# A third score buffer, token rows whole in DRAM, and a TensorE turn for the early expert slots

## The chip, the cores and the metric

The kernel runs on one core of a Trainium2 chip. Its time is device time in microseconds (us) of that core, and lower is better.

## The reference

Queries are mean-pooled in pairs before attention; the attention output, laid out as tokens, goes through a top-1 mixture of experts.

```python
B, H, S, D = (8, 8, 1152, 64)
q_pool = q.reshape(B, H, S // 2, 2, D).mean(axis=3)          # 576 queries
scores = (1 / sqrt(D)) * q_pool @ k.T                         # 576 x 1152 a head
attn = exp(scores - max); attn /= attn.sum(-1) + 1e-09
x = (attn @ v).transpose(0, 2, 1, 3).reshape(4608, 512)       # tokens
logits = x @ w_gate                                           # 8 experts
expert_idx = argmax(logits);  gate_w = softmax(logits)[expert_idx]
for e in range(8):                                            # 512 -> 1024 -> 512
    out[mask] = gate_w[mask] * (relu(x[mask] @ w1[e]) @ w2[e])
```

## The kernel before, in words

One Python class, `Flow`, plans the whole program. Each step is added with an engine, a cost in ns, a key (its due place), the steps it follows and the buffers it holds (`room` says how many of each kind there are). `Flow` plays the steps through with these costs and writes every engine's instructions in the order that comes out. On the chip each engine runs its own list in that order and waits at semaphores, so a step that waits holds up all that stands behind it on its engine.

**Attention** runs over 8 batches, in each over 4 pairs of heads, in each over 2 halves of 288 queries. A half is 9 chunks of 128 keys. For each chunk TensorE forms scores for both heads in a score buffer `st` of two PSUM banks (`product`, L516), and VectorE takes them to the tile `s` and finds their maxima in the same pass (`take`, L520); this frees the buffer. After the last chunk TensorE spreads the maxima into a further `st` buffer (L538), VectorE makes the bias (L544), ScalarE takes the exponential in three pieces (L548). The product with V collects 9 chunks in `pa`, two PSUM banks (L619); ScalarE and VectorE bring it to `xT` (L623, L624). For the softmax sums (`chunk_sum`) GpSimd folds nine chunks to two in three additions (L594) and TensorE adds those over the keys (L603), or, for the last half of a batch and for three pairs of the last batch, TensorE adds all nine (L589). All eight halves of a batch accumulate in one PSUM bank, `sums`. `row_sums` brings that bank to SBUF (ScalarE, L633), turns it (L639) and inverts it (L645, L646). `routing` computes logits, picks the expert, ranks tokens and scatters list entries (L793), in the same `sums` bank. PSUM has 8 banks: two `st` buffers of two, `pa` two, `sums` one, `m` one.

The rows of tokens go to DRAM in `x_runs`: a token's 512 values are four runs of 128 values and its factors, 528 bytes each. The four planes of runs lie one behind the other, so a token's runs are far apart. SyncE stores them with one DMA per third of a batch (L785).

**Experts** run in slots: 3 early ones (L818 onwards picks them after batch 6), 6 wide ones of 384 tokens, and a static rest. For a slot GpSimd loads its list (L877, L879), forms indices (L888; VectorE does for early slots) and gathers the runs, 128 runs an indirect DMA (L892), twelve for 384 tokens. VectorE multiplies by the softmax factors (L1051) and turns the tokens with a 32x32 block transpose (L1054), which with the four planes on four groups of partitions gives the transposed matrix; ScalarE and VectorE split it into a high and a low part, `xh` (L1058) and `xl` (L1015). Weights are split the same way (L1075, L1015). TensorE forms the hidden layer in three products (L1107) and the output in three (L1134); ScalarE scales it (L1146), GpSimd scatters it (L1141).

Of the kernel before, what the change touches and what calls it, by code (L numbers as in the profile page):

```python
# [9 lines left out]
F32 = mybir.dt.float32  # L10
# [12 lines left out]
S_BUFS = 2  # L23
BANKS = 5 - S_BUFS * 2
UNITS = 4
# [228 lines left out]
def kernel(  # L254
# [43 lines left out]
    planes = xg.rearrange("(g t) x -> g t x", g=NQD)  # L298
# [52 lines left out]
    for g in range(NQD):  # L351
        nc.vector.memset(gid[g * BL:(g + 1) * BL], float(g * (NT + 1)))
# [47 lines left out]
    def open_attention(exact, base, pairs, units):  # L400
# [3 lines left out]
        o.ps_m = base.enter_context(tc.tile_pool(name="ps_m", bufs=3 if exact else BANKS, space=PSUM))  # L404
# [19 lines left out]
    def turn_ns(n):  # L424
        return 60 + 1.25 * n
# [14 lines left out]
    def sum_bank(o):  # L440
        return hold_of("sums", lambda h: o.ps_m.tile([P, 512], F32, **h.own("sums", 1)))
# [57 lines left out]
    def scores(o, f, key, x, half, step=None):  # L499
# [8 lines left out]
        for c in range(NC):  # L508
            pt = hold_of("st", lambda h: o.ps_s.tile([P, 2, 512], F32, **h.own("st")))
# [15 lines left out]
            m = f.add("PE", 460, product, at, done(*x.q[half], *x.k.get(c, ())), [pt, s, x.kT, x.qT], QUADS)  # L525
            taken.append(f.add("DVE", 150 + dve(2 * HQ), take, at, done(m), [pt, s]))
# [5 lines left out]
        pb = hold_of("st", lambda h: o.ps_s.tile([P, 2, 512], F32, **h.own("st")))  # L532
# [45 lines left out]
    def chunk_sum(o, f, key, s, ready, b, hp, half, sums, last):  # L578


        key += K_SUM
        if not o.exact and (hp == NHP - 1 and half == 1 or b == B - 1 and hp >= NHP - LAST):

            def whole():
                for i in range(0, NC, 2):
                    for j in range(min(2, NC - i)):
                        for h in range(2):
                            to = slice(64 * j + 32 * h, 64 * j + 32 * h + 32)
                            nc.tensor.matmul(sums.t[to, :HQ], ones4[:, hp, half, :], s.t[:, i + j, h], start=False,  # L589
                                             stop=hp == NHP - 1 and half == 1 and i + j + 2 >= NC, tile_position=(0, to.start))  # L590

            return f.add("PE", 485 * (NC + 1) // 2, whole, key + 10, [*every(ready), *done(*last)], [s, sums], COLS)
        u = tile_of(o, "fold", [P, 3, 2, HQ], bufs=FOLD_BUFS, pool=o.rt)
        add = lambda to, a, b: nc.gpsimd.tensor_tensor(to, a, b, ALU.add)  # L594
        p = f.add("POOL", pool(6 * HQ), lambda: add(u.t, s.t[:, 0:3], s.t[:, 3:6]), key, every(ready[:6]), [s, u])
        p = f.add("POOL", pool(6 * HQ), lambda: add(u.t, u.t, s.t[:, 6:9]), key, done(p, *every(ready[6:])), [s, u])
        p = f.add("POOL", pool(2 * HQ), lambda: add(u.t[:, 0], u.t[:, 0], u.t[:, 2]), key, done(p), [u])

        def total():
            for i in range(2):  # L600
                for h in range(2):
                    to = slice(64 * i + 32 * h, 64 * i + 32 * h + 32)
                    nc.tensor.matmul(sums.t[to, :HQ], ones4[:, hp, half, :], u.t[:, i, h], start=hp == half == 0,  # L603
                                     stop=hp == NHP - 1 and half == 1, tile_position=(0, to.start))

        return f.add("PE", 500, total, key + 15, done(p, *last), [u, sums], COLS)

    def values(o, f, key, x, s, ready, hp, half, xT):
        pa = hold_of("pa", lambda h: o.ps_m.tile([P, 2, 512], F32, **h.own("pa", 1)))
# [3 lines left out]
        for c in range(NC):  # L613
# [8 lines left out]
            p = f.add("PE", 460, product, key + 20.0 * c / NC, done(p, x.v, ready[c]), [pa, x.vn, s], QUADS)  # L622
# [4 lines left out]
    def row_sums(o, f, key, sums, summed, rec, sm, end):  # L627

        key += K_ROW - end * 30
        if end and FILL:  # L630
            f.add("PE", 215 * FILL, lambda: [nc.tensor.matmul(
                sums.t[:, 3 * P:], ones, ones, start=True, stop=True) for _ in range(FILL)], key, summed, [sums])
        p = f.add("ACT", act(HQ) - 44, lambda: nc.scalar.copy(sm.t, sums.t[:, :HQ]), key, summed, [sums, sm])  # L633
# [3 lines left out]
        def turn():  # L637
            for j in range(HQ // QP):
                nc.tensor.matmul(sums.t[:QP, HQ + j * NS:HQ + (j + 1) * NS], sm.t[:, j * QP:(j + 1) * QP],  # L639
                                 sums_of.rearrange("p f a h -> p (f a h)"), start=True, stop=True)  # L640

        def inverse():

            src = sums.t[:QP, HQ:HQ + 3 * NS].rearrange("p (j f h) -> p f j h", j=3, f=2)
# [3 lines left out]
        p = f.add("PE", 500, turn, key, done(p), [sm, sums])  # L648
        return f.add("DVE", 600, inverse, key, done(p), [sums, rec])

    def attend(o, f, key, b, hp, xT, sums, summed):
# [3 lines left out]
        for half in range(2):  # L655
            at = key + 20 * half
            s, r = scores(o, f, at, x, half, EXPS)
            summed.append(chunk_sum(o, f, at + 20, s, r, b, hp, half, sums, summed[-1:]))
# [5 lines left out]
    def routing(o, f, key, b, xT, rec, sums, ready, hold=()):  # L664
# [18 lines left out]
        pl = pt = pr = sums  # L683

        aside = lambda at, n: pt.t[:QP, 3 * P + at:3 * P + at + n]
# [4 lines left out]
        def logits():  # L690
            for half in range(2):
                for a in range(NHP):
                    nc.tensor.matmul(
                        pl.t[32 * a:32 * a + 32, :HQ], wg[:, a, half, :], xT.t[:, a, half * HQ:(half + 1) * HQ],
# [524 lines left out]
    with tc.If(again > 0):  # L1219
        reset_state()  # L1220
        empty_lists()
        with ExitStack() as cm:
            o = open_attention(True, cm, cm, cm)
            with tc.For_i(0, B, 1) as b:
# [6 lines left out]
                for hp in range(NHP):  # L1231
                    attend(o, f, 0, b, hp, xT, sums, [])
# [49 lines left out]
```

## Time and profile before

| | us |
|---|---|
| median of 3 runs (range) | 1287.85 (1286.34 to 1294.69) |
| the profiled execution | 1292.46 |
| its span in the trace | 1290.9 |
| mean granted TensorE clock in it | 0.972 of full speed |

The span is what the trace covers; 1.56 us lie around it. The profiled execution is 4.6 us above the median. Attention fills the span to about 799 us, batch by batch, and the experts the rest.

### The profile page before, as it was taken

To read this page: it belongs to the slowest core of one execution; us is meant where nothing else is said; L and a number is where in the kernel's file an instruction comes from. 1 tells how busy PE (TensorE), PEld (TensorE's weight loads), DVE (VectorE), ACT (ScalarE), POOL (GpSimd) and SP (SyncE) were. 2 spreads that over 40 slices of the span, in tenths; PEclk is the share of its full clock that TensorE was granted. 3 is DMA by queue.
4 is the path that set the end of the run, shared out by engine and by line. 5 is a ranking of instruction groups with operands and counts; after the bars stand their busy time and mean duration, and the time that the engine had idled before them with its cause. 6 is when DMAs were issued, how large, how long until landed. Compare 5 with 4: busy or idle time off the path is not lost. (4 is left out here: it accounts for less than half of the span.)

```text
span 1290.9 us, 32856 instructions
## 1 busy us (share of the span) xinstructions
PE 1178.6 (91%) x13393; PEld 807.8 (63%) x13393; DVE 888.5 (69%) x2241; ACT 594.2 (46%) x688; POOL 809.3 (63%) x491
## 2 busy tenths in 40 slices
PE   4899999999999998999998496997999999999997
PEld 1455555455455454554554143886898899998986
DVE  5788877878878879788877243874556656566661
ACT  1455455445455445454552134443444444455551
POOL 0897699697795995996991622255887886421000
PEclk9899999999999999999999689998999999999999
DMA  9874446456456447555452301675566565566640
GB/s 146 127 116 88 104 66 108 99 92 96 83 92 107 88 83 125 76 89 111 76 94 82 110 18 40 159 224 148 175 186 185 176 181 173 159 223 193 232 149 20
DMA packets 379585, 158.12 MB, mean 122 GB/s; under 512 B 311012, under 2 KB 346780, under 8 KB 379424
## 3 DMA queue, kind: packets, MB, share of 16 engines
q1 hardware_dynamic: 367440, 135.10, 47.5%
q0 software_dynamic: 10896, 20.78, 5.8%
q8 instruction: 108, 1.77, 0.6%
q14 instruction: 53, 0.43, 0.1%
q10 hardware_dynamic: 1088, 0.03, 0.1%
HBM read 135.06 MB, written 22.07 MB: 122 GB/s over the span
## 5 line engine op out<-in xcount | busy, mean ns | idle before, releaser
L520 DVE TENSOR_SCALAR_CACHE_REDUCE s<-st 128x576 f32<-128x576 f32 x576 | 421.6, 750 | 138.2 <-PE st L516 118.6
L548 ACT ACTIVATE s<-s,bias 128x1728 f32<-128x1728 f32 x192 | 326.0, 1731 | 361.5 <-DVE bias L544 297.0
L516 PE MATMUL st<-qT,kT 64*64 64x288 f32 x4608 | 378.5, 417 | 55.7 <-DVE s L520 26.0
L619 PE MATMUL pa<-s,vn 64*64 64x288 f32 x4608 | 358.9, 406 | 4.1 <-issue 2.9
L516 PEld LDWEIGHTS st<-qT,kT 64*64 64x64 f32 x4608 | 161.1, 134 | 205.2 <-DVE s L520 86.6
L619 PEld LDWEIGHTS pa<-s,vn 64*64 64x64 f32 x4608 | 172.1, 134 | 107.5 <-issue 20.2
L594 POOL TENSOR_TENSOR fold<-s 128x1728 f32<-128x1728 f32 x51 | 197.0, 3869 | 22.9 <-ACT s L548 22.7
L594 POOL TENSOR_TENSOR fold<-fold,s 128x1728 f32<-128x1728 f32 x51 | 197.1, 3870 | 0.9
L1107 PE MATMUL ph<-xh,w1h 128*128 128x384 f32 (+1 forms) x512 | 163.4, 319 | 17.8 <-DVE hl L1115 8.2
L1107 PE MATMUL ph<-xl,w1h 128*128 128x384 f32 (+1 forms) x512 | 161.6, 316 | 0.2 <-DVE xl L1015 0.2
L1107 PE MATMUL ph<-xh,w1l 128*128 128x384 f32 (+1 forms) x512 | 161.3, 315 | 0.0
L892 POOL DMA_INDIRECT xr<-x_runs,ix x104 | 115.1, 1107 | 63.0 <-DVE ix L888 32.9
L1141 POOL DMA_INDIRECT out_dram<-y,rec x41 | 48.7, 1188 | 166.8 <-ACT y L1146 143.6
L1134 PE MATMUL py<-w2h,hh 128*128 128x512 f32 x328 | 128.2, 391 | 0.0
L1134 PE MATMUL py<-w2l,hh 128*128 128x512 f32 x328 | 127.9, 390 | 0.0
L1134 PE MATMUL py<-w2h,hl 128*128 128x512 f32 x328 | 127.9, 390 | 0.0
L793 POOL DMA_INDIRECT lists<-re,di x48 | 44.5, 928 | 131.5 <-DVE di L754 122.6
L1015 DVE TENSOR_TENSOR w2l<-raw,w2h 128x1024 fp32r<-128x1024 f32 x64 | 77.9, 1221 | 65.1 <-ACT w2h L1075 38.3
L1113 ACT ACTIVATE hh<-ph 128x384 fp32r<-128x384 f32 (+1 forms) x100 | 52.0, 521 | 137.1 <-PE ph L1107 108.9
L1107 PEld LDWEIGHTS ph<-xh,w1h 128*128 128x128 f32 x512 | 97.9, 191 | 22.6 <-DVE hl L1115 10.4
L1115 DVE SCALAR_TENSOR_TENSOR hl<-ph,hh 128x384 fp32r<-128x384 f32 (+1 forms) x100 | 59.1, 592 | 60.3 <-ACT hh L1113 50.6
L1107 PEld LDWEIGHTS ph<-xl,w1h 128*128 128x128 f32 x512 | 97.8, 191 | 1.3 <-DVE xl L1015 0.6
(172 smaller groups left out, 1358.3 us busy)
## 6 DMA issues: line engine op xcount, KB each, us to landing
raw<-in_moe_w_dram SPq DMA_DIRECT2D x128, 512.0 KB
kp<-in_k_dram SPq DMA_DIRECT2D x128, 144.0 KB
qn<-in_q_dram SPq DMA_DIRECT2D x128, 144.0 KB
vn<-in_v_dram SPq DMA_DIRECT2D x128, 144.0 KB
x_runs<-row SPq DMA_DIRECT2D x24, 396.0 KB
xr<-x_runs,ix POOLq DMA_INDIRECT x104
x_runs<-empty SPq DMA_DIRECT2D x4, 297.0 KB
xq<-x_runs,ix POOLq DMA_INDIRECT x60
```

The lines of the kernel that those rows point to most:

```text
L516: nc.tensor.matmul(pt.t[to, h, :HQ], x.kT.t[up, c * P + i * D:c * P + (i + 1) * D], x.qT.t[up, cols], start=True, stop=True, tile_position ...
L520: nc.vector.tensor_scalar(s.t[:, c], pt.t[:, :, :HQ], -SCALE, None, op0=ALU.mult, op1=ALU.min, accum_out=mx.t[:, c:c + 1],)
L548: nc.scalar.activation(s.t[:, c0:c0 + n], s.t[:, c0:c0 + n], AF.Exp, bias=bias.t, scale=-1.0)
L594: add = lambda to, a, b: nc.gpsimd.tensor_tensor(to, a, b, ALU.add)
L619: nc.tensor.matmul(pa.t[cs, i, :HQ], x.vn.t[up, h, c, :], s.t[up, c, h], start=c == 0, stop=c == NC - 1, tile_position=(up.start, cs.start))
L892: nc.gpsimd.indirect_dma_start(out=x.xr[i // NQD].t[:, i % NQD, :], out_offset=None, in_=xg, in_offset=bass.IndirectOffsetOnAxis(ap=x.ix.t ...
L1015: (nc.gpsimd if eng == "POOL" else nc.vector).tensor_tensor(lo, raw, hi.bitcast(F32), ALU.subtract)
L1107: nc.tensor.matmul(view()[:, i, :], a[:, c, fp], b[:, c, :n], start=c == 0 and k == 0, stop=c == NDC - 1 and k == 2)
L1113: a = f.add("ACT", act(nb * n) - 44, lambda fs=fs, view=view: nc.scalar.activation(hidden(m)[0][:, fs, :n], view(), AF.Relu), at - 20, don ...
L1115: d = f.add("DVE", dve(nb * n), lambda fs=fs, view=view: nc.vector.scalar_tensor_tensor(hidden(m)[1][:, fs, :n], view(), 0.0, hidden(m)[0] ...
L1134: nc.tensor.matmul(py.t, a[:, c, hs], b[:, c % 2, :], start=c == 0 and k == 0, stop=c == NFC - 1 and k == 2)
L1141: nc.gpsimd.indirect_dma_start(out=out, out_offset=bass.IndirectOffsetOnAxis(ap=x.re.t.bitcast(I32)[:, r, 0:1], axis=0), in_=y.t, in_offse ...
```

## The change

1. `S_BUFS` is 3. The two single banks `sums` and `m` are gone: 3 x 2 + 2 = 8 banks. Each half's sums now go to an `st` buffer of their own; ScalarE copies the first of a batch to SBUF (`sm`), VectorE adds the seven others there. `row_sums`, `routing` (save that of the last batch, which uses `pa`'s banks), the pick of the early slots and the warm-up hold an `st` buffer too. Planner costs change: a score or value product 460 to 485 ns, `take` by 150 less, and a few of routing's.
2. In `x_runs` a token's four runs lie side by side, 2112 bytes. A third of a batch is stored by four DMAs, one per plane. The other slots gather single runs as before, by index 4 x token + plane.
3. An early slot gathers whole rows, 128 tokens a gather, with the list's own entries as indices: three gathers for 384 tokens. The multiplication writes tokens in the order that suits a full transpose (`across`, L1085 of the new file); TensorE turns 128 tokens by four 128x128 transposes into PSUM (L1092); ScalarE (L1097) and VectorE split from there.
4. In a list load the half that the gather of single runs needs (`li`) now stands behind the other (`rec2`).

The core of the diff:

```diff
-S_BUFS = 2
-BANKS = 5 - S_BUFS * 2
+S_BUFS = 3
...
-    planes = xg.rearrange("(g t) x -> g t x", g=NQD)
+    planes = xg.rearrange("(t g) x -> g t x", g=NQD)
+    whole_rows = xg.rearrange("(t g) x -> t (g x)", g=NQD)
...
-            m = f.add("PE", 460, product, at, done(*x.q[half], *x.k.get(c, ())), [pt, s, x.kT, x.qT], QUADS)
-            taken.append(f.add("DVE", 150 + dve(2 * HQ), take, at, done(m), [pt, s]))
+            m = f.add("PE", 485, product, at, done(*x.q[half], *x.k.get(c, ())), [pt, s, x.kT, x.qT], QUADS)
+            taken.append(f.add("DVE", dve(2 * HQ), take, at, done(m), [pt, s]))
...
-    def chunk_sum(o, f, key, s, ready, b, hp, half, sums, last):
+    def chunk_sum(o, f, key, s, ready, b, hp, half, sm, last):
         key += K_SUM
+        ps = score_banks(o)
...
+                        nc.tensor.matmul(ps.t[to, 0, :HQ], ones4[:, hp, half, :], u.t[:, i, h], start=True,
+                                         stop=True, tile_position=(0, to.start))
+            p = f.add("PE", 500, total, key + 15, done(p), [u, ps], COLS)
+        if not last:
+            return f.add("ACT", act(HQ) - 44, lambda: nc.scalar.copy(sm.t, ps.t[:, 0, :HQ]), key + 15, done(p), [ps, sm])
+        return f.add("DVE", dve(HQ), lambda: nc.vector.tensor_tensor(sm.t, sm.t, ps.t[:, 0, :HQ], ALU.add),
+                     key + 15, done(p, *last), [ps, sm])
...
-        pl = pt = pr = sums
+        pl = pt = pr = value_banks(o) if b == B - 1 else score_banks(o)
...
-                nc.sync.dma_start(out=rows.rearrange("d (i g j) x -> g d i (j x)", g=NB, j=NJ)[g], in_=row.t.rearrange("p j x -> p (j x)"))
+                for d in range(NQD):
+                    nc.sync.dma_start(out=rows[d].rearrange("(i g j) x -> g i j x", g=NB, j=NJ)[g], in_=row.t[d * BL:(d + 1) * BL])
...
+        if early:
+            def fetch(r):
+                nc.gpsimd.indirect_dma_start(
+                    out=x.xr[r].t.rearrange("p b x -> p (b x)"), out_offset=None, in_=whole_rows,
+                    in_offset=bass.IndirectOffsetOnAxis(ap=x.re.t.bitcast(I32)[:, r, 0:1], axis=0),
...
+            if x.whole:
+                def across(r=r, feats=feats, xt=xt):
+                    nc.vector.tensor_tensor(xt.t.rearrange("p c (d i) -> p d c i", i=BL), feats(),
+                                            x.xr[r].t[:, :, P:].unsqueeze(3).broadcast_to([P, NQD, NDC, BL]), ALU.mult)
+                px = hold_of("py", lambda h: m.ps.tile([P, DM], F32, **h.own("py")))
+                def cross(xt=xt, px=px):
+                    for c in range(NDC):
+                        nc.tensor.transpose(px.t[:, c * P:(c + 1) * P], xt.t[:, c], ident)
+                made = lambda px=px: px.t.rearrange("p (c t) -> p c t", c=NDC)
+                p = f.add("DVE", dve(DM), across, key + r, x.rows[r:r + 1], [xt, x.xr[r]])
+                p = f.add("PE", 450, cross, key + r, done(p), [x.x, px, xt])
...
```

Three places of the instruction order. First TensorE in a steady stretch of the third batch (`st` score products, `pa` value products, four instructions a chunk). Before:

```order
L619 MATMUL pa_2665<-s_2292,vn_2087 64x288 x4
L516 MATMUL st_2706<-qT_2505,kT_2281 64x288 x4
L619 MATMUL pa_2665<-s_2292,vn_2087 64x288 x8
L516 MATMUL st_2730<-qT_2505,kT_2281 64x288 x4
L619 MATMUL pa_2665<-s_2292,vn_2087 64x288 x4
L538 MATMUL st_2742<-ident,top 64x64 x4
L619 MATMUL pa_2665<-s_2292,vn_2087 64x288 x8
L516 MATMUL st_2759<-qT_2505,kT_2281 64x288 x4
L516 MATMUL st_2764<-qT_2505,kT_2281 64x288 x4
```

and after, where `st_2579` and `st_2586` are the sums of two halves in score buffers:

```order
L519 MATMUL st_2523<-qT_2071,kT_2074 64x288 x4
L519 MATMUL st_2528<-qT_2071,kT_2074 64x288 x4
L519 MATMUL st_2534<-qT_2071,kT_2074 64x288 x4
L519 MATMUL st_2541<-qT_2071,kT_2074 64x288 x4
L519 MATMUL st_2547<-qT_2319,kT_2327 64x288 x4
L628 MATMUL pa_2553<-s_2198,vn_1853 64x288 x16
L608 MATMUL st_2579<-fold_2340,ones_73 32x288 x4
L593 MATMUL st_2586<-s_2198,ones_73 32x288 x18
L541 MATMUL st_2616<-ident,top 64x64 x4
L628 MATMUL pa_2553<-s_2198,vn_1853 64x288 x4
L519 MATMUL st_2628<-qT_2319,kT_2327 64x288 x4
```

Score products now stand up to five in a row, value products up to four, and the sums stand between them in the same ring of buffers.

Second GpSimd behind the list scatters of batch 6. Before (`xr`, `xq` are the gathered tiles):

```order
L892 DMA xr_8897<-x_runs,ix_8890 128x132 x4
L892 DMA xr_8973<-x_runs,ix_8890 128x132 x4
L892 DMA xr_9036<-x_runs,ix_8890 128x132 x4
L892 DMA xr_9110<-x_runs,ix_8906 128x132 x4
L892 DMA xr_9179<-x_runs,ix_8906 128x132 x4
L892 DMA xr_9242<-x_runs,ix_8906 128x132 x4
L892 DMA xr_9305<-x_runs,ix_9102 128x132 x4
L892 DMA xq_9456<-x_runs,ix_9102 128x132 x4
L892 DMA xq_9495<-x_runs,ix_9102 128x132 x4
```

and after:

```order
L903 DMA xr_9177<-x_runs,rec_0_8916 128x528
L903 DMA xr_9182<-x_runs,rec_0_8916 128x528
L903 DMA xr_9192<-x_runs,rec_0_8916 128x528
L903 DMA xr_9205<-x_runs,rec_1_8927 128x528
L903 DMA xr_9223<-x_runs,rec_1_8927 128x528
L903 DMA xr_9242<-x_runs,rec_1_8927 128x528
L903 DMA xr_9269<-x_runs,rec_2_8938 128x528
L903 DMA xq_9564<-x_runs,rec_2_8938 128x528
L903 DMA xq_9575<-x_runs,rec_2_8938 128x528
```

Thirty-six gathers have become nine, each of 128 whole rows.

Third ScalarE where attention ends. Before (`w1h`, `w2h` are high parts of weights, `xh` of the first slot's tokens):

```order
L1075 CAST w1h_9453<-raw_8761 128x1024
L1058 CAST xh<-xt_9451 128x4x128
L1058 CAST xh<-xt_9460 128x4x128
L1075 CAST w1h_9470<-raw_8771 128x1024
L1075 CAST w1h_9478<-raw_8778 128x1024
L1075 CAST w1h_9486<-raw_8790 128x1024
L1058 CAST xh<-xt_9481 128x4x128
L623 COPY xT_8432<-pa_9375 128x288
```

and after:

```order
L1123 CAST w1h_9561<-raw_8871 128x1024
L1123 CAST w1h_9570<-raw_8876 128x1024
L1123 CAST w1h_9580<-raw_8881 128x1024
L1123 CAST w1h_9583<-raw_8883 128x1024
L1123 CAST w2h_9587<-raw_8886 128x1024
L632 COPY xT_8629<-pa_9483 128x288
L1123 CAST w2h_9597<-raw_8900 128x1024
L1097 CAST xh<-py_9591 128x4x128
L1097 CAST xh<-py_9600 128x4x128
L1123 CAST w2h_9619<-raw_9516 128x1024
L1097 CAST xh<-py_9614 128x4x128
```

The first slot's tokens come behind six weight pieces and a copy, where one weight piece stood ahead of the first two and four ahead of the third. On TensorE the twelve transposes and the logits of the last batch now stand between the last value products and the first expert product; on GpSimd the first three list loads of the wide slots have moved from behind the third scatter of the first slot's output (L1141) to between the three scatters.

## Rows read from the trace of the kernel before

**Rows 1.** The page's first part: busy time of each engine over the whole span, its share of it, and its instructions.

```profile
PE 1178.6 (91%) x13393; PEld 807.8 (63%) x13393; DVE 888.5 (69%) x2241; ACT 594.2 (46%) x688; POOL 809.3 (63%) x491
```

**Rows 2.** Four stretches of 90 us, one batch of attention each (the first of the four, and their sum): length, busy time of each engine with its count of records, granted clock, DMA share.

```profile
320.00:410.00 90.00, 85.43 (x1348) 47.49 (x1343) 73.55 (x219) 45.62 (x48) 74.52 (x31) 0.98 0.54 95
...
sum 360.00, PE 339.56 PEld 189.07 DVE 294.15 ACT 182.16 POOL 297.95; mean PE 84.89 PEld 47.27 DVE 73.54 ACT 45.54 POOL 74.49
```

**Rows 3.** Waits from 120 to 680 us, a little over six batches: engine and line, what it waited for, us in total, times, longest.

```profile
DVE s L520 <- PE st L516: 87.5, 167, 2.1
PEld st L516 <- DVE s L520: 56.0, 100, 1.4
PE st L516 <- DVE s L520: 14.1, 32, 0.9
PE sums L603 <- POOL fold L594: 6.7, 13, 1.3
POOL lists L793 <- DVE di L754: 71.0, 6, 12.1
```

**Rows 4.** Groups of instructions by line, shapes apart: line, engine, operation, tiles, count | busy, mean ns of one | idle time before. The last row is the summary of line 785's DMA issues (ns min/median/max, first and last start).

```profile
L520 DVE TENSOR_SCALAR_CACHE_REDUCE s<-st 128x576 f32<-128x576 f32 x576 | 421.6, 750 | 138.2 <-PE st L516 118.6 <-remote 17.3 <-issue 0.4
L624 DVE TENSOR_TENSOR xT<-xT,pa 128x288 f32<-128x288 f32 x64 | 28.6, 447 | 10.3 <-ACT xT L623 7.9 <-issue 2.4
L892 POOL DMA_INDIRECT xr<-x_runs,ix x104 | 115.1, 1107 | 63.0 <-DVE ix L888 32.9 <-issue 29.0 <-POOL ix L888 0.6
L1141 POOL DMA_INDIRECT out_dram<-y,rec x41 | 48.7, 1188 | 166.8 <-ACT y L1146 143.6 <-issue 13.3 <-DVE xq L1051 6.1
L1058 ACT CAST xh<-xt 128x512 fp32r<-128x512 f32 x41 | 23.7, 618 | 4.5 <-issue 2.9 <-DVE xt L1054 1.5
L700 PE MATMUL sums<-ident,sm 128*96 128x128 f32 x24 | 4.3, 286 | 0.1
L785 SPq DMA_DIRECT2D x_runs<-row x24: 537/594/1864, 137.6 to 829.0; - x24
```

**Rows 5.** Stretches of the last batch and of the passage to the experts, columns as in rows 2.

```profile
690.00:698.00 8.00, 4.96 (x58) 2.36 (x55) 6.66 (x41) 1.47 (x1) 5.51 (x6) 1.00 0.05 8
718.00:751.00 33.00, 12.80 (x72) 4.14 (x72) 3.93 (x11) 3.46 (x3) 22.07 (x22) 0.57 0.22 48
751.00:773.00 22.00, 21.54 (x296) 10.29 (x292) 13.07 (x37) 7.33 (x6) 4.01 (x4) 0.94 0.06 14
773.00:785.00 12.00, 8.58 (x91) 3.37 (x83) 3.05 (x8) 5.39 (x4) 8.02 (x8) 1.00 0.22 46
799.00:805.00 6.00, 0.67 (x1) 0.29 (x1) 5.05 (x8) 6.00 (x9) 0.00 (x0) 0.69 0.37 90
805.00:880.00 75.00, 74.15 (x386) 66.23 (x386) 57.81 (x127) 37.23 (x62) 32.03 (x32) 0.98 0.67 179
```

**Rows 6.** Timelines of single engines from 715 to 752 us (start, length, engine, line, operation, tiles, count, and in brackets the idle time before it and its releaser): the first and the last of the 24 gathers of this burst, then VectorE and TensorE.

```profile
715.38 1.04 POOL L892 DMA_INDIRECT xr<-x_runs,ix  x1 [18.02 <-DVE ix L888]
...
745.51 1.00 POOL L892 DMA_INDIRECT xr<-x_runs,ix  x1 [0.30 <-issue]
...
742.61 0.29 DVE L544 TENSOR_REDUCE bias<-st 128x1 f32<-128x128 f32 x1 [13.45 <-remote]
...
722.20 0.34 PE L538 MATMUL st<-ident,top 64*64 64x64 f32 x8 [1.94 <-issue]
...
729.21 1.24 PE L516 MATMUL st<-qT,kT 64*64 64x288 f32 x8 [2.51 <-DVE s L520]
742.96 1.24 PE L516 MATMUL st<-qT,kT 64*64 64x288 f32 x8 [12.51 <-issue]
```

**Rows 7.** TensorE beside the last eight gathers of slot 2 (773 to 784 us), columns as in rows 6.

```profile
779.33 0.68 PE L589 MATMUL sums<-s,ones 128*32 128x288 f32 x3 [0.82 <-issue]
```

**Rows 8.** TensorE and ScalarE where attention ends and the experts begin, columns as in rows 6.

```profile
794.18 4.60 PE L619 MATMUL pa<-s,vn 64*64 64x288 f32 x72
...
798.84 1.04 ACT L1075 CAST w1h<-raw 128x1024 fp32r<-128x1024 f32 x1 [5.33 <-PE pa L619]
...
800.83 2.93 ACT L1075 CAST w1h<-raw 128x1024 fp32r<-128x1024 f32 x3
...
804.34 0.69 PE L1107 MATMUL ph<-xh,w1h 128*128 128x384 f32 x1 [5.56 <-ACT xh L1058]
...
809.72 0.64 PEld L693 LDWEIGHTS sums<-xT,wg 128*32 128x32 f32 x16 [0.25 <-issue]
```

**Rows 9.** GpSimd, VectorE and TensorE around the first slot that is not an early one, columns as in rows 6, and two stretches, columns as in rows 2.

```profile
851.92 1.49 POOL L1141 DMA_INDIRECT out_dram<-y,rec  x1 [6.09 <-DVE xq L1051]
853.52 0.79 POOL L877 DMA_DIRECT2D li<-lists  x1
...
861.13 1.09 POOL L892 DMA_INDIRECT xr<-x_runs,ix  x1 [0.31 <-issue]
...
883.13 0.69 DVE L1051 TENSOR_TENSOR xr<-xr 128x512 f32<-128x512 f32 x1 [4.38 <-DMA xr<-x_runs,ix]
...
885.48 0.69 PE L1107 MATMUL ph<-xh,w1h 128*128 128x384 f32 x1 [4.94 <-DVE hl L1115]
...
880.00:886.00 6.00, 1.06 (x6) 0.74 (x5) 2.87 (x5) 1.80 (x3) 0.00 (x0) 0.77 0.65 216
900.00:904.00 4.00, 2.04 (x6) 2.04 (x7) 2.78 (x4) 0.00 (x0) 3.09 (x4) 0.54 0.24 51
```

More of the change, by code (lines that the diff above doesn't have):

```diff
@@ L403, in open_attention @@
         o.wk = base.enter_context(tc.tile_pool(name="wk", bufs=1 if exact else 2))
-        o.ps_m = base.enter_context(tc.tile_pool(name="ps_m", bufs=3 if exact else BANKS, space=PSUM))
+        o.ps_m = base.enter_context(tc.tile_pool(name="ps_m", bufs=3 if exact else 1, space=PSUM))
         o.ld = pairs.enter_context(tc.tile_pool(name="ld", bufs=1))
@@ L588, in whole @@
                             to = slice(64 * j + 32 * h, 64 * j + 32 * h + 32)
[L589 to L604, printed above, removed]
@@ L606, in chunk_sum, with total @@
-        return f.add("PE", 500, total, key + 15, done(p, *last), [u, sums], COLS)
+                            nc.tensor.matmul(ps.t[to, 0, :HQ], ones4[:, hp, half, :], s.t[:, i + j, h], start=i == 0,
+                                             stop=i + j + 2 >= NC, tile_position=(0, to.start))
+            p = f.add("PE", 485 * (NC + 1) // 2, whole, key + 10, every(ready), [s, ps], COLS)
+        else:
+            u = tile_of(o, "fold", [P, 3, 2, HQ], bufs=FOLD_BUFS, pool=o.rt)
+            add = lambda to, a, b: nc.gpsimd.tensor_tensor(to, a, b, ALU.add)
+            p = f.add("POOL", pool(6 * HQ), lambda: add(u.t, s.t[:, 0:3], s.t[:, 3:6]), key, every(ready[:6]), [s, u])
+            p = f.add("POOL", pool(6 * HQ), lambda: add(u.t, u.t, s.t[:, 6:9]), key, done(p, *every(ready[6:])), [s, u])
+            p = f.add("POOL", pool(2 * HQ), lambda: add(u.t[:, 0], u.t[:, 0], u.t[:, 2]), key, done(p), [u])
+            def total():
+                for i in range(2):
+                    for h in range(2):
+                        to = slice(64 * i + 32 * h, 64 * i + 32 * h + 32)
+                        nc.tensor.matmul(ps.t[to, 0, :HQ], ones4[:, hp, half, :], u.t[:, i, h], start=True,
+                                         stop=True, tile_position=(0, to.start))
+            p = f.add("PE", 500, total, key + 15, done(p), [u, ps], COLS)
@@ L662, with routing @@
     stores = []
-    def routing(o, f, key, b, xT, rec, sums, ready, hold=()):
+    def routing(o, f, key, b, xT, rec, ready, hold=()):
         wk = o.wk
@@ L929, in upto @@
             return cum
[L931 removed]
+        pb, left = value_banks(o), small("left", NE)
         last = done(f.add("PE", 60, lambda: nc.tensor.matmul(
[L933 removed]
+            pb.t[0:1, 0, :NE], ones_bf[:, 0:1], cnt, start=True, stop=True), key, last, [pb]))
         tu = small("tu", NE)
@@ L1181 @@
             key = PAIR * (b * NHP + NHP)
-            outs.append(row_sums(o, f, key, sums, done(*summed), rec, sm, b == B - 1))
-            outs = routing(o, f, key, b, xT, rec, sums, outs, hold)
+            outs.append(row_sums(o, f, key, sm, done(*summed), rec, b == B - 1))
+            outs = routing(o, f, key, b, xT, rec, outs, hold)
             if b == B - 2:
```

139 lines of the change are left out of this document (77 added, 62 removed).

## The prediction

> **What bounds the kernel now.** I read the busy times first, then the stretches of steady attention, the waits in them, and last the places where TensorE's records thin out. The busy times [rows 1] show TensorE at 91% of the span, so a gain has to come from the 112 us in which it is idle, or from work taken off it. The stretches say where these lie. A steady batch takes 90.0 us with TensorE busy for 84.9, VectorE for 73.5 and GpSimd for 74.5 [rows 2]: 5.1 us idle a batch. About 1345 matmul records fall in 90 us, 14.9 a us; this pace is my gauge for the last batch.
>
> The waits of six and a fifth batches name what the 5.1 us are [rows 3]. VectorE waits for scores and TensorE for the release of a score buffer, in turns: with two buffers each is often one step behind the other. On TensorE itself the wait for VectorE's `take` is 14.1 us (2.3 a batch) and the wait of the sums for the folds 6.7 us (1.1 a batch). The 56.0 us of the weight loads overlap with products still running and are no loss of their own. GpSimd's 71.0 us for the list scatters are slack: it is idle there, and its busy 74.5 of 90 leave room.
>
> The last batch is another picture. While 24 gathers leave GpSimd back to back (715.38 to 746.5 us, 1.0 us each and 0.3 between), TensorE gets 72 records through in 33 us, where the pace gives 492 [rows 5]. That is 4.8 us of work and 28.2 us lost. Nobody waits for data there: the maxima were spread at 722.2, VectorE reduced them only at 742.61 after an idle time put down to no engine of the program, and TensorE's product at 742.96 stands behind 12.51 us of plain issue [rows 6]. The next 22 us, with four more gathers, hold 296 records (19.9 us of work, 2.1 lost), and the 12 us of the last eight gathers hold 91 (6.1 us, 5.9 lost) [rows 5]; there TensorE proceeds by three or four matmuls and 0.8 us of issue in turn, at the gathers' own pitch [rows 7]. Together 36.2 us beside 36 gathers: 1.0 each. The six list scatters at 690 to 698, which move next to nothing (DMA share 0.05), show the same: 58 records where 119 were due, 4.1 us [rows 5]. So the loss goes with the number of indirect DMAs in a row rather than with their bytes. Against that reading stands the experts' stretch 805 to 880, where GpSimd is busy 32 us with such work and TensorE is busy 74.15 of 75 [rows 5]; but its records are larger, five a us instead of fifteen.
>
> **The change part by part.** *A, the third score buffer.* It can remove the 2.3 and the 1.1 us a batch, 3.4 of 5.1. It costs VectorE seven additions a batch; the nearest row is the addition of `xT`, 128x288 from PSUM, 447 ns [rows 4]: 3.1 us, which makes 76.6 of 90 busy. They stand between the takes, whose own length of 0.75 [rows 4] is well under the time of a score and a value chunk on TensorE (144 chunks in 84.9 us, 1.2 for two), so about half of each is felt. I take -3.4 + 1.5, near -2 a batch, and seven batches without the gathers: -14. Bounds: -30 (all but 0.8 us of the idle time) and +7 (the additions felt wholly, a third of the waits still there). ScalarE's copy of the sums moves to the first half of a batch, and ScalarE is idle for half of each batch: nothing.
>
> *B, 9 gathers for 36.* By the count, 27 gathers fewer give back 27 us. A gather of 128 rows of 2 KB has a near relation in the output scatter, 1188 ns against 1107 [rows 4], so the nine left cost 9 x 1.07 = 9.7, and 36.2 - 9.7 = 26.5; some of what is given back meets the batch's usual 6% of idle time: -25. Bounds: 0 (it follows the bytes, which stay the same) and -32 (nine gathers cost hardly anything). Nothing else is late in the place of these gathers: slot 0's tokens are wanted only at 799, and even now the last gather of slot 2 has left by 785 [rows 5].
>
> *C, list loads moved ahead.* Behind the third scatter (851.92) GpSimd now spends until 861.13 on list loads and indices before the first gather of a wide slot; the wide tokens arrive at 883.13, VectorE waits 4.38 for them, and TensorE 4.94 [rows 9]. In the new order three of the loads precede, so the first gather leaves up to 7.7 us (861.13 less 853.41) earlier. That takes away the 4.94, and the 2 us that the next products lose at the lower clock (0.77 in that stretch, and 0.54 again at 900 to 904): -7, bounds 0 (the scatters themselves wait for their data as late as now) and -12.
>
> *D, attention to experts.* Now the first product starts 5.56 us after the last value product [rows 8], with one weight piece and two `xh` ahead of it. In the new order ScalarE does one weight piece in 1.04 and five in 0.98, a copy in about 0.4, two `xh` in 0.62 each [rows 4, 8], another weight and the last `xh`: 9.2 us, with 0.5 for VectorE's low part behind it, 9.7. That is 4.1 later. The last batch's logits, 1.18 us of TensorE [rows 8], and twelve transposes fall into that gap for nothing; -1.2. The clock, granted at 0.69 in the present gap [rows 5], stays low a little longer: +0.5. Sum +3.5, bounds +2 and +6.
>
> *E, the transposes of slots 1 and 2* stand on a TensorE that is busy: 24 of them. The nearest row is the transposes of the logits, 24 in 4.3 us busy, 286 ns for a single one [rows 4]: +4, bounds +3 and +7. VectorE's nine block transposes that go, and its nine multiplications in another order, lie beside other work: nothing. The Trainium skill speaks against this part: "TensorE: Matmul & The Clock Gate", Part 4: PE-mode transpose, gives about 275 ns for a 128x128 transpose in a kernel's context, and says that the result lies in PSUM, from where a copy has to fetch it. By that figure 24 would be an estimated 6.6 us and the whole sum 2.6 us worse; the row's 286 ns is the single duration, and its 4.3 us for 24 show that neighbours overlap.
>
> *F, row stores.* 96 DMAs in place of 24 at 594 ns of SyncE each [rows 4], 43 us more over some 700 on a queue that only issues; pieces of 528 bytes in place of 3168 with the DMA engines busy by 0.54 [rows 2]. The weight loads queued behind them on SyncE have a whole batch of time. Nothing, bounds 0 and +3.
>
> The sum on the profiled execution: -14 - 25 - 7 + 3.5 + 4 = -38.5, so 1292.46 becomes 1254. That execution was 4.6 us above the median of the runs, so I predict 1249.
>
> **The rivals.**
> *Rival 1: the dead time is not cut (1274).* If the stall follows the bytes or the elements written, which stay at 1152 rows of 2112 bytes, B is 0, and the sum is -13.5. For it: the clean case of the count, the scatters, loses 0.7 each and not 1.0. Against it: the pitch of rows 7 is one gather, and DMA is at 0.22 in the worst stretch [rows 5]. The Trainium skill gives this rival weight: "Runtime: NRT & Kernel Launch", Instruction fetch mechanics, has each engine fetch its next block of instructions by a DMA queue of its own while it executes, mostly hidden, and "DMA: Bandwidth & Descriptors", Queues, rings and completion order, has each DMA engine switch between queues after every packet. By these a burst of gathers would hold up no other engine; the trace shows VectorE and TensorE held up together [rows 6], so here the rule does not hold as it stands.
>
> *Rival 2: the third buffer gives nothing (1263).* The sums of each half and routing take buffers from the same ring; for a good part of a batch routing holds one, and two are left as before. Then A is 0 and the rest stays: -24.5. For it: the order shows sums in the middle of the ring. Against it: a sum holds its buffer for one addition, not for 0.97 us of a chunk pair.
>
> *Rival 3, slower: VectorE sets the pace of the score runs (1299).* Score products now come five in a row, which TensorE can do at 0.49 us each (four concurrent products of 417 ns that start one behind another), while a take needs 0.68 to 0.75 [rows 4]. In a run of five, VectorE falls behind by (5 - 2) x 0.2 = 0.6 us a half, 4.8 a batch; with the sums' additions in the ring felt whole (3.1), less the 3.4 saved, a batch grows by 4.5 instead of falling by 2: 8 x 4.5 = 36. With B to E the sum is -24.5 + 36 = +11.5. It decides if the value products behind a run are too short to let VectorE catch up; four in a row are 1.9 us and three takes 2.1. Against it: over a half VectorE has 9 takes in 11 us and is busy 0.82 [rows 2].
>
> *Rival 4: everything to its bound (1230).* A at -30 and B at -28 give -58.
>
> **How the numbers follow.** My forecast of 1249 has 0.52, rival 1 0.22, rival 2 0.12, rival 3 0.09, rival 4 0.05. One per cent of 1287.85, about what a measurement of this kernel can tell from no change, is 13 us: below 1275 is faster. Forecast, rivals 2 and 4 are faster (0.69) save for the edge of the forecast's own bounds; rival 1 lies on the border and is split. That gives 0.77 faster, 0.14 within, 0.09 slower. The range has to leave out no more than 2 in 10: rival 3 stays out, half of rival 4 and the far ends of rival 1 too: 1230 to 1280.
>
> **What would show it.** Steady batches of 88 us, with TensorE's waits for `take` under 1 us a batch; a batch of 90 or more refutes A, and VectorE's share tells rival 2 from 3. In the last batch nine gathers within some 12 us and no stretch of 10 us under a quarter of the pace (B); if TensorE is as thin for 30 us with GpSimd idle, rival 1 holds. First expert product 9 to 10 us after the last value product (D). No TensorE gap of 5 us at the first wide slot (C). What would make all of it wrong: the dead time is set by where a fetch of instructions falls, which moves with every change of the order.

## The result, and the profile after

The changed kernel takes 1253.46 us (median of 4, 1251.74 to 1257.82) against 1291.27 (1286.34 to 1295.61): a ratio of 0.9715, 95% interval 0.9687 to 0.9742. The profiled execution took 1253.06 us, its span is 1251.4. The forecast was 1249 with 1230 to 1280, made against a median of 1287.85.

Busy times of the page, which answer to [rows 1], then the same steady stretches as in [rows 2] (first and sum), then the waits from 120 to 660 us that answer to [rows 3] (a little over six batches in both):

```profile
PE 1176.7 (94%) x13429; PEld 808.1 (65%) x13429; DVE 911.1 (73%) x2285; ACT 595.7 (48%) x688; POOL 781.0 (62%) x464
```

```profile
320.00:410.00 90.00, 86.77 (x1352) 47.73 (x1350) 78.44 (x231) 46.05 (x48) 76.26 (x32) 0.98 0.55 97
...
sum 360.00, PE 347.56 PEld 191.46 DVE 313.75 ACT 183.10 POOL 294.82; mean PE 86.89 PEld 47.87 DVE 78.44 ACT 45.77 POOL 73.71
```

```profile
PEld st L519 <- DVE s L523: 51.2, 101, 1.4
DVE s L523 <- PE st L519: 42.0, 139, 0.9
...
PE st L519 <- DVE de L760: 9.7, 6, 1.6
...
PE st L519 <- DVE s L523: 6.4, 14, 0.7
```

TensorE is busy as long as before (1176.7 and 1178.6 us) in a span 39.5 us shorter. In steady attention its wait for `take` has halved (14.1 to 6.4 us), the wait of the sums for the folds has left the head of the list, and a new one stands there, 9.7 us for routing's use of a score buffer.

The span is best split at five marks on TensorE's timeline, before (first two rows, with [rows 8] for the two marks between them) and after (the rest): row sums of batch 6, end of the last value products, first expert product, last expert product, end.

```profile
665.62 0.68 PE L639 MATMUL sums<-sums_of,sm 128*96 128x16 f32 x6
...
1280.92 0.39 PE L1134 MATMUL py<-w2h,hl 128*128 128x512 f32 x1
```

```profile
210.50 0.68 PE L648 MATMUL st<-sums_of,sm 128*96 128x16 f32 x6
...
653.79 0.68 PE L648 MATMUL st<-sums_of,sm 128*96 128x16 f32 x6
...
749.45 4.60 PE L628 MATMUL pa<-s,vn 64*64 64x288 f32 x72
753.98 1.09 PE L1092 MATMUL py<-ident,xt 128*128 128x128 f32 x8
761.54 1.09 PE L1092 MATMUL py<-ident,xt 128*128 128x128 f32 x4 [6.47 <-DVE xl L1042]
762.56 2.11 PE L702 MATMUL pa<-xT,wg 128*32 128x288 f32 x16
764.59 0.44 PE L1155 MATMUL ph<-xh,w1h 128*128 128x384 f32 x1
...
1234.32 0.39 PE L1182 MATMUL py<-w2h,hl 128*128 128x512 f32 x1
```

| stretch | before | after | difference |
|---|---|---|---|
| start to row sums of batch 6 | 665.62 | 653.79 | -11.8 |
| to the end of the last value products (the gauge below) | 133.2 | 100.3 | -32.9 |
| to the first expert product | 5.6 | 10.5 | +5.0 |
| to the end of the last expert product | 477.0 | 470.1 | -6.9 |
| to the end of the span | 9.6 | 16.7 | +7.1 |

Five steady batches lie between the row sums at 210.50 and 653.79, 88.7 us each, where a batch took 90.0. Around the early gathers the stretch that answers to [rows 5] is this, and TensorE's timeline beside it answers to [rows 7]:

```profile
702.00:712.00 10.00, 8.63 (x96) 3.51 (x89) 2.26 (x9) 4.99 (x3) 7.07 (x7) 1.00 0.55 143
```

```profile
708.76 0.73 PE L628 MATMUL pa<-s,vn 64*64 64x288 f32 x5 [0.32 <-issue]
710.17 1.14 PE L519 MATMUL st<-qT,kT 64*64 64x288 f32 x5 [0.68 <-issue]
```

Seven whole-row gathers leave in these 10 us, and TensorE gets 96 records through where 149 would be the pace: the same stepping at about the gathers' pitch, beside nine gathers instead of 36.

### The profile page after: what moved, and what is told of

Its sections match the earlier page's. It is cut to its first block, busy times and chain, and to the rows that moved or that the text cites. A ratio compares the mean times of both kernels' runs of the same rounds, so it can differ in the third digit from the quotient of the medians.

```text
span 1251.4 us, 33147 instructions
## 1 busy us (share of the span) xinstructions
PE 1176.7 (94%) x13429; PEld 808.1 (65%) x13429; DVE 911.1 (73%) x2285; ACT 595.7 (48%) x688; POOL 781.0 (62%) x464
## 5 line engine op out<-in xcount | busy, mean ns | idle before, releaser
L551 ACT ACTIVATE s<-s,bias 128x1728 f32<-128x1728 f32 x192 | 320.0, 1726 | 339.1 <-DVE bias L547 339.1
L523 DVE TENSOR_SCALAR_CACHE_REDUCE s<-st 128x576 f32<-128x576 f32 x576 | 416.6, 750 | 76.7 <-PE st L519 54.7
L519 PE MATMUL st<-qT,kT 64*64 64x288 f32 x4608 | 382.8, 423 | 40.7 <-DVE qT L487 11.8
L628 PE MATMUL pa<-s,vn 64*64 64x288 f32 x4608 | 351.3, 405 | 0.7 <-issue 0.6
L519 PEld LDWEIGHTS st<-qT,kT 64*64 64x64 f32 x4608 | 164.7, 136 | 191.2 <-DVE s L523 74.1
L1189 POOL DMA_INDIRECT out_dram<-y,rec x41 | 45.1, 1099 | 158.4 <-ACT y L1194 147.1
L919 POOL DMA_INDIRECT xr<-x_runs,ix x76 | 87.4, 1150 | 23.5 <-issue 21.6
L1155 PEld LDWEIGHTS ph<-xh,w1l 128*128 128x128 f32 x512 | 96.4, 188 | 0.0
```

Source lines behind the costliest of these rows:

```text
L519: nc.tensor.matmul(pt.t[to, h, :HQ], x.kT.t[up, c * P + i * D:c * P + (i + 1) * D], x.qT.t[up, cols], start=True, stop=True, tile_position ...
L523: nc.vector.tensor_scalar(s.t[:, c], pt.t[:, :, :HQ], -SCALE, None, op0=ALU.mult, op1=ALU.min, accum_out=mx.t[:, c:c + 1],)
L551: nc.scalar.activation(s.t[:, c0:c0 + n], s.t[:, c0:c0 + n], AF.Exp, bias=bias.t, scale=-1.0)
L628: nc.tensor.matmul(pa.t[cs, i, :HQ], x.vn.t[up, h, c, :], s.t[up, c, h], start=c == 0, stop=c == NC - 1, tile_position=(up.start, cs.start))
L919: nc.gpsimd.indirect_dma_start(out=x.xr[i // NQD].t[:, i % NQD, :], out_offset=None, in_=xg, in_offset=bass.IndirectOffsetOnAxis(ap=x.ix.t ...
L1155: nc.tensor.matmul(view()[:, i, :], a[:, c, fp], b[:, c, :n], start=c == 0 and k == 0, stop=c == NDC - 1 and k == 2)
```

## The experiments

**Was the dead time the number of gathers, their bytes, or something else?** Four variants of the changed kernel, all in the changed kernel's own order of instructions. Each replaces only what the step `fetch` issues (in short, not in the code's words):

```diff
e1/f1: for i in range(4): gather 32 rows into xr[r].t[32*i:32*i+32], indices of partitions 0 to 31
e2/f2: for d in range(4): gather 128 runs into xr[r].t[:, d], index 4 * token + d
e5:    nc.sync.dma_start(out=xr[r], in_=whole_rows[(3*s+r)*128 : (3*s+r+1)*128])
e6:    + behind each gather: 3 x nc.gpsimd.tensor_tensor(idle, idle, idle, ALU.add)     # 128 x 576
```

> The changed kernel with each early gather of 128 rows split into four of 32 whole rows: 36 indirect DMAs again, the same bytes, the same 1152 descriptors of 2112 bytes. It leaves out three quarters of the early slots' tokens: all four take the indices of the first 32 partitions. Gauge: the time from the row sums of batch 6 to the end of the last value product, 133.2 us before and 100.3 after. If the dead time goes with the number of indirect DMAs (my theory), it comes back at about 1.0 us for each of the 27 more: gauge near 127, time near 1280. If it goes with the bytes, or with the number of runs fetched, nothing changes: gauge near 100, time near 1253.

> The changed kernel with its early slots fetched as before, by 36 gathers of 128 runs of 528 bytes (index 4 x token + plane, made by four small operations a slot on GpSimd), the transposes by TensorE kept. Number of indirect DMAs: gauge near 127, time near 1280, as for the split into 32 rows. Number of runs (4608 in place of 1152): the same here, but not there. Bytes: 1253.

> The changed kernel with its nine early gathers replaced by nine plain DMAs of 128 rows from SyncE's queue: no indirect gather is left in attention. It leaves out the choice of the early slots' tokens (it loads the first 1152). If what is left of the dead time beside the nine gathers is theirs (9.7 us by the prediction), the gauge falls from 100.3 to 91 to 94 and the time to 1244 to 1247. If the rest is not theirs (the list scatters and the pick of the slots alone), it stays at 99 to 101 and 1253.

> The changed kernel with three idle additions of 1.4 us on GpSimd behind each of the nine early gathers, which puts 4.2 us between two of them. If each gather costs its 1.0 us wherever it stands, nothing changes: gauge near 100, time 1253. If only gathers back to back cost (rival: the list scatters of steady batches stand between folds and nobody misses anything there), the gauge falls to 92 to 95 and the time to 1246.

These four ran on one chip, and there the kernel before took 1245.76 us (21 runs, 1241.1 to 1251.93), 45 less than where the change was first measured. There is no trace of the kernel before from that chip, so that its own dead time is missing there is inferred from its time. The four took 1239.69, 1236.40, 1241.65 and 1236.92 (ratios 0.9943, 0.9912, 0.9968, 0.9932), with gauges of 89.7, 90.4, 90.4 and 89.7. No theory expected that: thirty-six gathers in a row, of either form, cost no more there than nine spaced ones or none. TensorE beside 36 gathers of 128 runs on that chip:

```profile
700.00:710.00 10.00, 10.00 (x168) 5.62 (x168) 7.74 (x24) 5.85 (x6) 7.62 (x11) 1.00 0.19 44
710.00:720.00 10.00, 10.00 (x168) 5.78 (x160) 5.08 (x14) 1.42 (x1) 7.59 (x12) 1.00 0.21 48
```

Next both kernels, unchanged, on another chip:

> The kernel before, unchanged, for its trace beside the kernel's other runs here. In the first four experiments the kernel before took 1246 us beside them, 45 us less than where the change was first measured, and 36 gathers in a row did not slow TensorE. If the dead time of the first measurement belongs to the chip or the hour and not to the gathers, this trace shows about 1345 matmul records in 90 us through the gathers as well, and the gauge from batch 6's row sums to the last value product is 95 to 100 us, not 133. If the dead time comes from these gathers in this program alone, it is there again and something else is 45 us shorter.

> The changed kernel, unchanged, beside it. If the dead time is gone from the kernel before, the whole of term B is gone here, and what is left of the sum is A, C, D and E: by the first pair of traces -11.8 to the row sums of batch 6, +5 at the passage, -6.9 in the experts, the tail aside: about -14, or 1232 for 1246. If the change still took 32 us off there, 1213.

The dead time was back: the kernel before took 1293.29 (median of 9), with 72, 289 and 99 records in the three stretches of [rows 5] that held 72, 296 and 91, and the changed kernel 1256.12, ratio 0.972 (0.9694 to 0.9747). Their gauges are 135.4 and 100.0. At the five marks of the table above this pair differs by -10.9, -35.4, +5.0, -8.9 and +6.8, which shows how far such differences repeat. Then the two forms of 36 gathers once more, on yet another chip, where the kernel before took 1291.14:

> The split into 36 gathers of 32 rows once more. The first time it ran beside a kernel before of 1246 us, where nothing stalled; on two other occasions the kernel before took 1288 to 1299 with the dead time in its trace. If the kernel before takes 1290 here too: by the number of indirect DMAs the gauge is near 127 and the time near 1282; by bytes or by the number of runs it stays at 100 and 1255. If the kernel before takes 1246 here, it tells nothing of that: gauge 90. It leaves out three quarters of the early slots' tokens, as before.

> The 36 gathers of 128 runs once more, with the same condition. If the kernel before takes 1290 here: by the number of indirect DMAs and by the number of runs alike, gauge near 127 and time near 1282; by bytes 100 and 1255. With the split into 32 rows this tells number of DMAs (both slow), number of runs (only this one slow) and bytes (neither) apart. A fourth reading, that the dead time needs the old layout of DRAM with its runs far apart, gives 100 for both as well.

They took 1288.11 and 1280.24 (one execution each), with gauges of 130.9 and 134.4. The program of the two rows above (128 runs), in the same two stretches:

```profile
700.00:710.00 10.00, 8.09 (x99) 3.83 (x91) 2.35 (x8) 4.99 (x3) 7.66 (x11) 1.00 0.18 42
710.00:720.00 10.00, 7.67 (x22) 2.03 (x21) 0.77 (x3) 0.00 (x0) 7.59 (x12) 0.55 0.22 49
```

GpSimd does the same in both; TensorE passes 22 records in 10 us instead of 168, VectorE 3 instead of 14. Both forms are slow with the same bytes as nine gathers, and one of them with the same 1152 descriptors: on such a chip it is the number of indirect DMAs, at (130.9 - 100.1) / 27 = 1.14 and (134.4 - 100.1) / 27 = 1.27 us each, where 100.1 is the mean of the changed kernel's two gauges. Bytes, runs and the old layout are out. The prediction's last doubt, that the place of an instruction fetch decides, is not excluded but unlikely: the dead time stands beside the gathers in four programs with different instructions.

**Third buffer, additions and planner costs.** One kernel has the additions without the buffer, the other the whole change with the old costs (the first edit in short; of the second only two of its costs are shown):

```diff
e3 (kernel before):
-    sums.t[to, :HQ] accumulated over the batch
+    ps = bank(o)   # own bank; ScalarE copies the first, VectorE adds the others to sm
e4 (changed kernel):
-    f.add("PE", 485, product, ...)      -    f.add("DVE", dve(2 * HQ), take, ...)
+    f.add("PE", 460, product, ...)      +    f.add("DVE", 150 + dve(2 * HQ), take, ...)
...
```

> The kernel before with one part of the change: each half's sums go to a bank of their own and are added by VectorE, with two score buffers as before. This is the price of the additions without the third buffer. If about half of each addition is felt (my step), a steady batch grows from 90.0 by 1.5 less the 1.1 of the sums' wait: 90 to 91, the time +0 to +8. If they are felt whole, 92 and +16. If they are hidden, 89 and -8.

> The changed kernel with the planner's costs of before (score and value products 460, take with 150 more, turns, and routing's). If the gain of a steady batch (90.0 to 88.7) is the third buffer's, it stays: 88 to 89. If it comes from the order that the new costs make, the batch goes back to 90 or more and the time rises by 9 or more.

They took 1327.13 (ratio 1.0264, 1.0227 to 1.0302) and 1271.07 (0.9835, 0.9805 to 0.9866). The five steady batches, row sums to row sums, first of e3, then of e4:

```profile
222.89 0.68 PE L644 MATMUL sums<-sums_of,sm 128*96 128x16 f32 x6
...
699.99 0.68 PE L644 MATMUL sums<-sums_of,sm 128*96 128x16 f32 x6
```

```profile
215.63 0.68 PE L648 MATMUL st<-sums_of,sm 128*96 128x16 f32 x6
...
671.68 0.68 PE L648 MATMUL st<-sums_of,sm 128*96 128x16 f32 x6
```

95.4 us a batch with two buffers and the additions, 91.2 with three and the old costs, 88.5 to 88.7 with three and the new ones, 90.0 before. The new costs are thus worth 2.6 us a batch as a whole. As prices of the parts one would read 5.4 for the additions and 4.2 back for the buffer, but e4 differs from e3 in the DRAM layout and in routing's use of the ring too, and the traces put most of these differences elsewhere. The five batches in the kernel before, e3, e4 and the changed kernel, columns as in [rows 2]:

```profile
215.67:665.62 449.95, 423.90 (x6705) 236.39 (x6701) 367.56 (x1096) 227.86 (x236) 372.52 (x155) 0.99 0.54 95
222.89:699.99 477.10, 441.01 (x6704) 236.43 (x6700) 395.60 (x1130) 227.51 (x236) 374.03 (x155) 0.96 0.51 89
215.63:671.68 456.05, 434.83 (x6705) 247.60 (x6701) 393.36 (x1130) 228.25 (x236) 374.29 (x156) 0.97 0.55 92
210.50:653.79 443.29, 429.00 (x6705) 237.07 (x6701) 387.01 (x1130) 229.09 (x236) 374.64 (x156) 0.98 0.56 94
```

The same number of records keeps TensorE busy for 17.1 us longer in e3 than before, 10.9 in e4, 5.1 in the changed kernel, and the granted clock falls with it. Of e3's 5.4 us a batch, 3.4 are products at a lower clock and 2.0 idle time. Cut each batch of some 1340 records at the 335th and the 470th, between which routing runs (means of the five, us):

| | before | e3 | e4 | changed |
|---|---|---|---|---|
| to the 335th record | 22.7 | 22.0 | 21.8 | 21.4 |
| to the 470th | 11.6 | 17.5 | 14.2 | 12.6 |
| to the next row sums | 55.7 | 56.0 | 55.2 | 54.7 |

All that e3 and e4 lose lies in the middle stretch. In the two others together the additions alone cost nothing that shows (-0.4), and e4 and the changed kernel gain 1.4 and 2.4. The loss begins at one VectorE instruction of routing on 96x6 values, `tok` or `re`. First its durations in the kernel before, e3, e4 and the changed kernel (ns min/median/max, first and last start), then the place in e3:

```profile
L760 DVE TENSOR_SCALAR tok<-tok x6: 160/160/161, 240.6 to 690.7; 96x6 f32<-96x6 f32 x6
L765 DVE TENSOR_SCALAR tok<-tok x5: 2878/2882/3037, 249.0 to 630.7; 96x6 f32<-96x6 f32 x5
L755 DVE CAST re<-tok x6: 168/2658/2841, 237.3 to 693.5; 96x6 int32<-96x6 f32 x6
L769 DVE TENSOR_SCALAR tok<-tok x6: 277/1348/1356, 235.5 to 677.6; 96x6 f32<-96x6 f32 x6
```

```profile
248.14 3.84 POOL L596 TENSOR_TENSOR fold<-s 128x1728 f32<-128x1728 f32 x1 [2.53 <-ACT s L548]
248.97 3.04 DVE L765 TENSOR_SCALAR tok<-tok 96x6 f32<-96x6 f32 x1
...
253.20 1.24 PE L516 MATMUL st<-qT,kT 64*64 64x288 f32 x8 [3.70 <-DVE s L520]
...
252.40:259.20 6.80, 5.63 (x47) 2.60 (x51) 4.90 (x14) 0.00 (x0) 6.18 (x4) 0.50 0.16 34
```

Where no fold runs beside it, as in the kernel before, it takes 0.16 to 0.28 us. Where GpSimd is in a fold, it ends 0.02 to 0.03 us behind that fold (251.98 and 252.01 here), in each of the five batches of e3, e4 and the changed kernel. In e3 the next take stands behind it, TensorE is idle for 3.70 us, and then the granted clock is 0.50, the lower of its two levels (1.2 GHz), for 6.8 us, once in each batch; in the changed kernel it is once 3.4 us, in the kernel before twice 3.4 in five batches. So what e3 and e4 lose is mainly set by where the planner's order puts `tok` and `re`. No run changes that place alone, so its price is read from the traces and not tested.

**The passage, and the nine gathers left.** Two changes of the changed kernel, on a chip where the kernel before took 1289.03:

```diff
e8:
-                      key + step * j, done(got[j]), [raw[j], w[j]])
+                      key + step * j, done(got[j], *(x.turned[::2] if x.lead and j else ())), [raw[j], w[j]])
...
e9: e8, and the three idle additions behind each early gather, as in e6
```

> The changed kernel with the first slot's weight pieces 2 to 4 of w1 held back in the planner until its tokens are split, so that ScalarE does one w1 piece, one w2 piece, a copy and then the tokens. The gap from the last value product to the first expert product was 10.54 us in the changed kernel and 5.56 before. By the order of ScalarE's list it falls to 6.5 to 7.5 and the time by 3 to 4. Rival: the gap was not on the path to the end, since TensorE then waits for the other three weight pieces: no change within 1 us. With a kernel before of 1290: 1250 against 1254.

> The same, with three idle additions of 1.4 us on GpSimd behind each early gather. Where the kernel before takes 1290, each of the 27 more gathers cost 1.1 to 1.25 us, so the nine left should cost about 11 of the gauge's 100. If each costs that wherever it stands, the gauge stays at 100 and the time at that of the run beside it. If it is gathers in a row that cost, the gauge falls to 89 to 93 and the time by 7 to 11. Where the kernel before takes 1246, both gauges are 90.

They took 1249.25 (ratio 0.9677, 0.9649 to 0.9706) and 1242.52 (0.9630, 0.9603 to 0.9656). The passage in e8:

```profile
751.72 4.59 PE L628 MATMUL pa<-s,vn 64*64 64x288 f32 x72
756.24 1.09 PE L1093 MATMUL py<-ident,xt 128*128 128x128 f32 x8
760.33 2.15 PE L702 MATMUL pa<-xT,wg 128*32 128x288 f32 x16 [2.99 <-DVE xT L633]
762.40 1.12 PE L1093 MATMUL py<-ident,xt 128*128 128x128 f32 x4
...
764.20 0.69 PE L1156 MATMUL ph<-xh,w1h 128*128 128x384 f32 x1
...
792.54 0.50 PE L1183 MATMUL py<-w2h,hh 128*128 128x512 f32 x1 [1.76 <-DVE xl L1043]
```

The gap is 7.9 instead of 10.5 us. That these 2.6 reach the end is not shown. At 792.54 TensorE waits 1.76 us, where the changed kernel waits 0.36, and the 151st expert product starts 44.9 us behind the last value product, against 44.0 and 45.3 in the changed kernel's two traces: by then the lead is gone. First to last expert product takes 470.1, against 470.1 and 473.1 there, and the changed kernel did not run on this chip. In e9 the gathers stand 4.8 us apart, and TensorE beside them:

```profile
702.00:712.00 10.00, 10.00 (x176) 5.91 (x170) 6.76 (x20) 5.27 (x4) 8.07 (x8) 1.00 0.23 62
712.00:732.00 20.00, 20.00 (x326) 11.18 (x322) 10.46 (x30) 8.86 (x7) 18.66 (x17) 1.00 0.21 57
```

Full pace; the gauge is 91.5 against 100.4 in e8, and the time 6.7 us less, a little under the 7 to 11 expected. The nine in a row thus cost 8.9 us, 1.0 each, and standing alone they cost nearly nothing: it is gathers in a row that hold the engines up. e9 is 3.7% under the kernel before.

## Why the prediction was right, step by step

The forecast of 1254 for the profiled execution met 1253.06, but its terms came out differently and cancelled: the signs and most of the mechanisms held, and that the sum hits to 1 us is luck.

*A (-14) measured -11.8*, and by another sum. Of it 5.2 us are there by the row sums of the second batch (215.67 and 210.50), and five steady batches give 1.3 each where I had forecast 2. TensorE's idle time fell by 2.4 us a batch (26.1 to 14.3 over five), and the lower clock took 1.0 back, which the prediction did not have. The additions are priced right by themselves (line 614, 442 ns); that half of each is felt, as I assumed, does not show: outside routing e3 is no slower than the kernel before. What I missed is that every change of the order moves `tok` and `re` against GpSimd's folds, and that TensorE's clock falls behind the wait that this makes. The order that the new costs make avoids the longest of these waits and is worth 2.6 us a batch, more than the term's 2, and the prediction did not price it at all. Rival 3 had VectorE holding up TensorE in runs of five score products; no run shows that as the cause. Rival 2 describes e4, whose batches gained nothing and which took 22 us off.

*B (-25) measured -32.9*, and -35.4 in the second pair, just outside the bound of -32; both include what A gives in the last batch. The reading by number held where the dead time exists, at 1.14 to 1.27 us a gather instead of 1.0, which makes 31 to 34 for 27. Rival 1, by bytes, fell with f1. The step that failed is the sentence that the loss goes with the number of indirect DMAs as such: on one chip 36 cost nothing, and 9 with other work between them cost nearly nothing where nine in a row cost 8.9. On the one chip the change is worth little: no run put it beside the kernel before there, but its spaced form had 0.9932. The two pages of the Trainium skill that I set against the reading ("Runtime: NRT & Kernel Launch", Instruction fetch mechanics; "DMA: Bandwidth & Descriptors", Queues, rings and completion order) would have a burst hold up nobody; the chip of the first four experiments agrees, every other session doesn't. What it is in a chip, or in the hour, that makes the difference stays open; the spared chip was seen in one session only.

*C and E (-7 + 4) measured -6.9 together*, -8.9 in the second pair, of which 1.2 are the logits that moved ahead. The first wide gather now leaves straight behind the third scatter, as forecast, and TensorE waits 2.59 us at that slot instead of 4.94:

```profile
804.07 2.11 POOL L1189 DMA_INDIRECT out_dram<-y,rec  x1 [0.30 <-DMA raw<-in_moe_w_dram]
806.49 1.09 POOL L919 DMA_INDIRECT xr<-x_runs,ix  x1 [0.30 <-issue]
```

```profile
844.42 0.44 PE L1155 MATMUL ph<-xh,w1h 128*128 128x384 f32 x1 [2.59 <-DVE hl L1163]
```

But the 4.94 belong to one execution: in the second trace of the kernel before the same product waits 0.66, and its longest waits in the experts, 3.57 and 5.64 us, stand at later products. One execution's wait was too narrow a ground for the term; what both pairs share is that the longest such wait falls, from 4.94 and 5.64 to 2.59 and 2.54. A group of four transposes lies between expert products with 0.60 us, six of them 3.6:

```profile
820.48 0.60 PE L1092 MATMUL py<-ident,xt 128*128 128x128 f32 x4
```

That is 0.15 each, near the 0.18 of the row that I used and below the 275 ns that the Trainium skill gives for a bf16 transpose in a kernel's context ("TensorE: Matmul & The Clock Gate", Part 4: PE-mode transpose); these are float32. Undoing the move of the list loads alone was not tried, so how C and E share the rest is argued, not shown.

*D (+3.5) measured +5.0.* The order of ScalarE's list made the delay, as worked out, and e8 shows that the gap follows that order, though not that closing it shortens the whole. Mis-sized were the third block of tokens, which waits for VectorE behind four weight pieces (6.47 us idle), and the logits, which fell into the low clock behind that idle time (granted 0.52 from 761.54 to 764.59, near the lower level of 1.2 GHz): 2.11 instead of 1.18.

*Not foreseen: +7.1 behind the last expert product*, 9.6 us before and 16.7 after. Of the kernel's work only the last scaling and scatter run there; the rest is the closing of the program, and 4.4 of the 7.1 are one closing instruction of GpSimd, its longest DRAIN, before and after (columns as for `tok`, times in ns):

```profile
L1277 POOLq DRAIN  x3: 46/103/2035, 1288.0 to 1290.6; - x3
L1325 POOLq DRAIN  x3: 46/103/6445, 1244.1 to 1251.1; - x3
```

It goes with the program and not with the chip: the programs with 36 gathers of 128 runs (the kernel before, e3, and that form of the changed kernel on both of its chips) have 2.04 and end 9.6 to 10.8 us behind the last product, all others 6.2 to 7.0 and 15.8 to 17.1. So the form of the early gathers decides this too; by what way is open.

## What to carry to other kernels

A stretch in which several engines thin out together while no tile is late is worth reading against GpSimd's timeline: if indirect DMAs leave it back to back, fetch whole rows with fewer of them, or put other work between. Test that on more than one chip, because a gain of 33 us on one can be nothing on the next. An instruction that is added moves all others of its engine, and a small one that comes to stand beside another engine's long one can cost more than the addition: look for an instruction that takes far longer than others of its shape, and at the granted clock behind it. A planner's costs are part of such a change and want an experiment of their own.

## What the runs showed of the hardware

The same program, with GpSimd's instructions at the same pitch of 1.3 us, lets TensorE pass 168 records in 10 us on one chip and 22 on another. Back to back an indirect DMA cost the other engines 1.0 to 1.3 us there, 4.8 us apart little that the gauge shows (91.5 against 89.7 to 90.4 where nothing stalls). It does not depend on bytes: 32 whole rows and 128 runs, both 67.6 KB, cost 1.14 and 1.27, and 128 whole rows, 270 KB, cost 1.0 and left GpSimd in 1.01 us. A VectorE instruction on 96x6 values takes 0.16 us alone and up to 3.04 beside a fold on GpSimd, and then it ends with that fold.
